# Windowed attention and two MLPs on one core: stores over two queues, exchanged accumulation banks, and three changes of order

## The chip, the core and the metric

The kernel runs on one core of one Trainium2 chip. A core has the engines TensorE (PE in the profile, its weight loads PEld), VectorE (DVE), ScalarE (ACT), GpSimd (POOL) and SyncE (SP), which here only issues transfers. Engines work side by side and wait for each other by semaphores; each takes its own instructions in order. The metric is the device time of one execution in microseconds, lower is better.

## The reference, cut to what matters

```python
def _attn_ref(q, k, v):                      # batch 4, heads 8, seq 576, head_dim 64
    scores = scale * np.matmul(q, k.transpose(0, 1, 3, 2))
    bias = slopes[:, None, None] * (-np.abs(rel))[None]
    mask = (rel >= 0) & (rel < 128)          # rel = query position - key position
    scores = np.where(mask, scores + bias[None], -1e9)
    attn = softmax(scores)
    return np.matmul(attn, v)

x = attention output, one row of 512 for each of the 2304 tokens
h = x @ w_in;  x = where(h > 0, h, exp(min(h, 0)) - 1) @ w_out      # first MLP, 512 -> 2048 -> 512
h = x @ w_in2; out = maximum(0.01 * h, h) @ w_out2                  # second MLP
```

## The kernel before, in words

**Numbers.** All MLP products are made of three matmuls with operands split in a high and a low part (`split_mm`), so that float32 accuracy is kept. The weights are split on the chip, one piece of 128 hidden columns at a time, by steps on ACT and DVE (`w_a1` to `w_lo`, lines 162 to 196): `w_hi` is the cast on ACT (line 189), `w_lo` two subtractions on DVE.

**Attention.** The 2304 tokens are nine blocks of 256, the heads four pairs. A pair of a block is two *steps*; a step is a tile of 128 queries (or tiles of 64 where a sequence of 576 ends and the next begins, in the blocks 2, 6 and 7) with both heads. A step goes: score matmuls, `score_min` on DVE (bias, row minimum, the two halves of the window folded into one), `score_exp` on ACT, `score_rec` (reciprocal) on DVE, `score_norm` on POOL (tile `t`), `transposes` on TensorE into a bank and a copy of it by ACT to tile `pt` (two buffers), `selects` on POOL (the folded part is split again into previous and own keys, in `pt`), `values` on TensorE into `av_ps`, then `values_cast` on ACT and `values_rest` on DVE, which make the high and low part of the MLP's input `x`.

**Banks.** PSUM has eight banks of 512 float32 columns, named by tags here: `y0` to `y3` (sums of the MLP's second product), `s0` and `s1` (scores), `h` and `c`. In the first MLP the hidden sums `h_ps` go alternately into `h` and `c` by the parity of the chunk, transposes into `s1` and `h`, the attention output `av_ps` into `c`.

**Opening** (lines 583 to 616). The first 16 steps run before any MLP work, in an order that is kept as written on every engine (`Ordered`). In round n: the transposes of step n, the values of step n-1, scores of step n+3, the reciprocal of step n+1, the minimum of step n+2, the normalization of step n+1, the exponentials of step n+2, the selects of step n. Up to round 13 the normalization stands ahead of the selects on POOL's queue; in rounds 14 and 15 behind them. Between them stand weight steps of the first pieces (`EARLY`).

**First MLP** (lines 631 to 651). The tokens are five blocks J (512, 256, 512, 512, 512). A block goes through 16 chunks c of 128 hidden columns: `mlp1_h` makes h (12 matmuls, then exponential on ACT, and minimum, maximum, cast and remainder on DVE and ACT), and two chunks later `mlp1_y` adds it into the four sums y. During the blocks 0 to 3, chunks in `starts` also carry attention for a later block: the transposes of a new pair of steps, the values of the pair before, selects, and the scores of the pair after. These are the chunks 3, 7, 11 and 15 of block 0 and every even chunk of the blocks 1 to 3. From here on a scheduler orders the instructions of ACT, DVE, POOL and SP; TensorE keeps the written order.

**End of a block.** The four sums y are copied to `ys` (odd ones by DVE, even ones by ACT; three buffers under tag `eg`, which the activations of both MLPs use too) and stored to `x2T` in DRAM, from where the second MLP loads them. The stores are issued by SP for the first three blocks and by ACT for the last two. Block 4 runs interleaved with the first chunks of the second MLP, whose first activation is `g` (line 681).

Of the kernel before, what the change touches and what calls it, by code (L numbers as in the profile page):

```python
# [20 lines left out]
B, H, S, D = 4, 8, 576, 64  # L21
# [24 lines left out]
FIRST = 16  # L46
# [38 lines left out]
def attention_elu_leaky_kernel(  # L85
# [11 lines left out]
    nc = tc.nc  # L97
# [158 lines left out]
    steps = []  # L256
# [186 lines left out]
    def values(s):  # L443
        if s >= NS:
            return
        st = steps[s]
        j, p = st["j"], st["p"]
        _, v, chunks = QKV[j, p]
        J = max(i for i, (t0, _) in enumerate(BLK1) if t0 <= j * BLK)
        if st["first"] and p == 0 and j * BLK == BLK1[J][0]:  # L450
            x1 = x1p.tile([P, 2, NK, 2 * BLK], F32R, tag="x1", name="x1")
            X1[J] = x1[:, 0], x1[:, 1]
        xh, xl = X1[J]

        early = j < RAW
        pt = st["pt"]
        if st["first"]:
            AV[p] = psp.tile([P, 512], F32, tag=f"y{p % 2}" if early else "c", name="av_ps")
        av, off = AV[p], -j * BLK
        mms = []  # L460
        for t0, n, hh, k0, nk, c in st["parts"]:
            ch = [x[0] for x in chunks].index(k0)
            nth = sum(x[0] == -nk and x[2] == hh for x in mms)
            mms.append((-nk, nth, hh, ch, slice(t0 + off, t0 + off + n), c))


        mms.sort(key=lambda x: x[:3])
        for i, (nk, _, hh, ch, q, c) in enumerate(mms):
            matmul(av[hh * D:hh * D + D, q], v[:-nk, ch, hh * D:hh * D + D], pt[:-nk, c],
                   start=st["first"] and all(x[2] != hh for x in mms[:i]),  # L470
                   stop=st["last"] and all(x[2] != hh for x in mms[i + 1:]), skip_group_check=True)
        st["out"] = None
        if st["last"]:
            o = slice(j * BLK - BLK1[J][0], j * BLK + BLK - BLK1[J][0])
            st["out"] = xh[:, p, o], xl[:, p, o], av[:, :BLK]
# [12 lines left out]
    def mlp1_h(J, cs, late_work=lambda: None):  # L488

        n = BLK1[J][1]
        xh, xl = X1[J]

        last = J == len(BLK1) - 1
        tag = "s0" if last and cs[0] < LAG2 and (LAG2 - cs[0]) % 2 else "h"
        if not last and cs[0] % 2 == (J == 0):

            tag = "c"  # L500
        ps = psp.tile([P, len(cs), n], F32, tag=tag, name="h_ps")
        ws = [weights(1, c, 0) for c in cs]

        late = NK - 1 if cs[0] == 0 else NK
        order = [(ci, kk) for ci in range(len(cs)) for kk in range(late)]
        order += [(ci, kk) for ci in range(len(cs)) for kk in range(late, NK)]
        for ci, kk in order:
            wih, wil = ws[ci]
            s = slice(kk * P, (kk + 1) * P)
            if (ci, kk) == (0, late):  # L510
                late_work()

            split_mm(ps[:, ci, :], wih[:, s], wil[:, s], xh[:, kk, :n], xl[:, kk, :n],
                     ci == 0 and kk == 0, kk == NK - 1, skip_group_check=True)

        g, hi, lo = (pool.tile([P, 2 * BLK], dt, tag=t, name=t)
                     for pool, t, dt in ((egp, "eg", F32), (glp, "gh", F32R), (glp, "gl", F32R)))
        ps = ps.rearrange("p c n -> p (c n)")
        m = len(cs) * n
        nc.scalar.activation(g[:, :m], ps, AF.Exp)  # L520
        nc.vector.tensor_scalar(g[:, :m], g[:, :m], 1.0, -1.0, op0=ALU.min, op1=ALU.add)  # L521
        nc.vector.tensor_tensor(g[:, :m], ps, g[:, :m], op=ALU.max)  # L522
        nc.scalar.copy(hi[:, :m], g[:, :m])  # L523
        nc.vector.tensor_tensor(lo[:, :m], g[:, :m], hi[:, :m].bitcast(F32), op=ALU.subtract)  # L524
        return hi, lo
# [3 lines left out]
    def mlp1_y(J, cs, gg):  # L529
        gh, gl = gg  # L530
        t0, n = BLK1[J]
        per = 512 // n
        if cs[0] == 0:
            Y[J] = [psp.tile([P, per, n], F32, tag=f"y{i}", name=f"y{i}") for i in range(NK // per)]
        for ci, i, m in [(ci, i, m) for ci in range(len(cs)) for i in range(3) for m in range(NK)]:
            woh, wol = weights(1, cs[ci], 1)
            w, g = ((woh, gh), (woh, gl), (wol, gh))[i]

            matmul(Y[J][m // per][:, m % per, :], w[:, m * P:(m + 1) * P], g[:, ci * n:ci * n + n],
                             start=cs[ci] == 0 and i == 0 and m % per == 0, stop=cs[ci] == NC - 1 and i == 2,  # L540
                             skip_group_check=True)
        if cs[-1] == NC - 1:
            for i, y in enumerate(Y.pop(J)):
                ys = egp.tile([P, per, n], F32, tag="eg", name="ys")
                if i % 2:
                    nc.vector.tensor_copy(ys, y)  # L546
                else:
                    nc.scalar.copy(ys, y)

                q = nc.sync if J < len(BLK1) - 2 else nc.scalar  # L550
                q.dma_start(out=x2T[:, i * per:i * per + per, t0:t0 + n], in_=ys)


# [40 lines left out]
    for n in range(FIRST):  # L594
        m = n + 2
        transposes(n, "ch"[n % 2])
        values_to(n - 1)
        if n + 3 < FIRST + 2:
            score_mm(n + 3)
        score_rec(m - 1)  # L600
        if n >= 2:
            values_cast(n - 2)
        score_min(m)
        if n < FIRST - 2:
            score_norm(m - 1)
        score_exp(m)
        selects(n)
        if n >= FIRST - 2:
            score_norm(m - 1)
        if n >= 2:  # L610
            values_rest(n - 2)
        w_early(n)
# [15 lines left out]
    for J in range(len(BLK1) - 1):  # L628
        t0, n = BLK1[J + 1]
        todo = NPAIR * (t0 + n) // BLK - done  # L630
        starts = [i * NC // todo + (3 if J == 0 else 0) for i in range(todo)]
        for c in range(NC):
            if c in starts:
                transposes(2 * done + 1, "s1")
                transposes(2 * done, "h")
                values_to(2 * done - 1)
                if J == 0:

                    w_tick(NC)
                for i in (1, 0):  # L640
                    selects(2 * done + i)
                scores(done + 1)
                done += 1
            elif c == 0 and J:
                values_to(2 * done - 1)
            g = mlp1_h(J, [c], first_late if c == 0 and J == 0 else lambda: None)
            if len(pend) == Y_LAG:
                mlp1_y(*pend.pop(0))
            if at["c"] < NC and c + 1 not in starts:
                w_tick(NC)  # L650
            pend.append((J, [c], g))
# [152 lines left out]
```

## Time and profile before

| | us |
|---|---|
| median of three runs | 944.99 (943.14 to 945.45) |
| the profiled execution, whole | 949.66 |
| its span, first to last instruction | 948.0 |
| TensorE busy | 923.8 (97%) |
| DVE busy | 408.8 (43%) |
| ACT busy | 405.0 (43%) |
| POOL busy | 115.6 (12%) |
| mean granted clock of TensorE | 0.988 of full speed |

All times in the views count from the start of the span. [...] A busy share is an average over stages: the opening lasts until about 47 us, the first MLP with attention until about 450, the first MLP's last block with the beginning of the second MLP until about 590, and the rest is the second MLP alone. A row of the timeline merges like instructions that follow each other; `x12` is their number, and what stands in brackets is how long the engine stood idle before them and what it then waited for.

### The profile page before, as it was taken

The numbers are of one execution on the slowest core, as the hardware profiler recorded it, in microseconds if no ns is written. First come the engines' busy times: TensorE is split into PE (matmuls) and PEld (weight loads), VectorE is DVE, ScalarE is ACT, GpSimd is POOL, SyncE is SP. The second block draws the span as 40 slices with busy tenths as digits, with TensorE's granted clock in tenths as the row PEclk, the third lists the DMA queues.
The fourth block names the chain that finished last, engine by engine and source line by source line (L and its number), as shares of the span: only waits on it lengthen the run. The fifth ranks groups of instructions, "written<-read, shape, count | busy, mean of one in ns | idle before, by whom it ended". The sixth has DMA issues, their size and how long they took to land.

```text
span 948.0 us, 12963 instructions
## 1 busy us (share of the span) xinstructions
PE 923.8 (97%) x4885; PEld 752.4 (79%) x4885; DVE 408.8 (43%) x1035; ACT 405.0 (43%) x918; POOL 115.6 (12%) x281
## 2 busy tenths in 40 slices
PE   8799999999999999999999998999999999999998
PEld 5468887998877777787888887888888888888886
DVE  5878965656544444443476665211211121111111
ACT  6877864444343443332376665322322232222222
POOL 4611122322222211221000000000000000000000
PEclk9979999999999999999999998999999999999999
DMA  9940422321210120100444334010110010001001
GB/s 287 353 174 16 141 67 69 89 67 49 65 45 23 43 82 27 46 9 1 156 157 146 124 128 157 1 67 1 45 44 1 1 45 1 0 1 45 1 1 45
DMA packets 41759, 66.77 MB, mean 70 GB/s; under 512 B 3680, under 2 KB 27232, under 8 KB 41696
## 3 DMA queue, kind: packets, MB, share of 16 engines
q1 hardware_dynamic: 40400, 63.72, 20.2%
q10 hardware_dynamic: 1296, 2.23, 0.6%
q8 instruction: 38, 0.62, 0.3%
q14 instruction: 25, 0.20, 0.1%
HBM read 56.49 MB, written 9.44 MB: 70 GB/s over the span
## 4 chain that ended last, share of the span: by engine, by line
PE 90%; ACT 3%; DMA 3%; DVE 2%; issue 1%; SPq 1%; POOL 0%; ACTq 0%; DVEq 0%
PE h_ps L120 42%; PE y L120 20%; PE o_y L120 18%; PE av_ps L120 3%; PE s_ps L120 2%; DMA wraw<-in_w_in 2%; PE pt_ps L411 2%; PE o_s L120 1%; PE o_c L120 1%; ACT pt L417 1%; DVE x L111 1%; DMA x2T<-ys 1%; ACT wraw L175 0%; ACT x L111 0%; ACT t L111 0%
## 5 line engine op out<-in xcount | busy, mean ns | idle before, releaser
L120 PE MATMUL h_ps<-x,w 128*128 128x512 f32 (+1 forms) x1920 | 431.4, 374 | 8.8 <-DVE x L111 3.7
L120 PEld LDWEIGHTS h_ps<-x,w 128*128 128x128 f32 x1920 | 340.0, 191 | 80.7 <-DVE x L111 12.2
L686 DVE TENSOR_TENSOR g2l<-g,g2h 128x512 fp32r<-128x512 f32 (+1 forms) x80 | 51.0, 637 | 270.1 <-ACT g2h L685 270.1
L120 PE MATMUL o_y<-w,g2h 128*128 128x512 f32 x512 | 157.9, 389 | 0.0
L120 PE MATMUL y<-gh,w 128*128 128x512 f32 (+1 forms) x640 | 157.5, 368 | 0.0
L681 ACT ACTIVATE g<-h_ps 128x512 f32<-128x512 f32 (+1 forms) x80 | 44.2, 554 | 255.9 <-PE h_ps L120 255.9
L120 PEld LDWEIGHTS y<-gh,w 128*128 128x128 f32 x640 | 113.9, 189 | 20.4 <-DVE ys L546 0.3
L120 PEld LDWEIGHTS o_y<-w,g2h 128*128 128x128 f32 x512 | 96.4, 188 | 20.1
L120 PE MATMUL o_y<-w,g2l 128*128 128x512 f32 x256 | 99.6, 389 | 0.0
L520 ACT ACTIVATE eg<-h_ps 128x512 f32<-128x512 f32 (+1 forms) x80 | 44.0, 551 | 88.8 <-PE h_ps L120 86.2
L111 ACT ACTIVATE t<-t,stat 128x128 f32<-128x128 f32 (+2 forms) x160 | 62.6, 394 | 45.3 <-DVE t L111 30.3
L111 POOL TENSOR_SCALAR t<-t,stat 128x128 f32<-128x128 f32 (+3 forms) x160 | 66.9, 431 | 101.1 <-DVE stat L111 91.3
L120 PE MATMUL y<-gl,w 128*128 128x512 f32 (+1 forms) x320 | 78.7, 368 | 0.0
L523 ACT CAST gh<-eg 128x512 fp32r<-128x512 f32 (+1 forms) x80 | 46.2, 578 | 74.2 <-DVE eg L522 67.5
L111 POOL TENSOR_SCALAR_AFFINE_SELECT pt<-pt 128x256 f32<-128x256 f32 (+1 forms) x112 | 47.2, 429 | 221.0 <-ACT pt L417 217.2
L524 DVE TENSOR_TENSOR gl<-eg,gh 128x512 fp32r<-128x512 f32 (+1 forms) x80 | 51.3, 641 | 38.8 <-ACT gh L523 38.6
L120 PEld LDWEIGHTS y<-gl,w 128*128 128x128 f32 x320 | 56.9, 189 | 10.0
L521 DVE TENSOR_SCALAR eg<-eg 128x512 f32<-128x512 f32 (+1 forms) x80 | 32.6, 408 | 72.1 <-ACT eg L520 70.1
L120 PEld LDWEIGHTS o_y<-w,g2l 128*128 128x128 f32 x256 | 48.0, 188 | 10.0
L111 DVE CUSTOM_DVE_ANT_0 t<-s_ps,bias 128x256 f32<-128x256 f32 (+4 forms) x160 | 51.8, 370 | 2.9 <-PE s_ps L120 2.8
L522 DVE TENSOR_TENSOR eg<-h_ps,eg 128x512 f32<-128x512 f32 (+1 forms) x80 | 50.9, 638 | 2.5
L685 ACT CAST g2h<-g 128x512 fp32r<-128x512 f32 (+1 forms) x80 | 46.3, 578 | 2.3
(58 smaller groups left out, 678.7 us busy)
## 6 DMA issues: line engine op xcount, KB each, us to landing
wraw<-in_w_in SPq DMA_DIRECT2D x32, 512.0 KB, 3.8
wraw<-in_w_out SPq DMA_DIRECT2D x32, 512.0 KB, 4.8
qkr<-in_kT SPq DMA_DIRECT2D x28, 192.0 KB, 2.9
xr<-x2T SPq DMA_DIRECT2D x4, 1024.0 KB, 5.4
qkr<-in_qT SPq DMA_DIRECT2D x28, 128.0 KB, 2.6
out<-os SPq DMA_DIRECT2D x14, 256.0 KB, 2.2
vr<-in_vp SPq DMA_DIRECT2D x16, 192.0 KB, 2.5
x2T<-ys SPq DMA_DIRECT2D x10, 256.0 KB, 2.3
```

The source lines that it names most:

```text
L111: ins = f(*args, **kw)
L120: tc.keep_in_program_order(nc.tensor.matmul(*args, **kw))
L411: tc.keep_in_program_order(nc.tensor.transpose(ps[:nk, col:col + n], t[:n, c:c + nk], ident[:n, :n]))
L417: tc.keep_in_program_order(nc.scalar.copy(pt[:nk, c], ps[:nk, c]))
L520: nc.scalar.activation(g[:, :m], ps, AF.Exp)
L521: nc.vector.tensor_scalar(g[:, :m], g[:, :m], 1.0, -1.0, op0=ALU.min, op1=ALU.add)
L522: nc.vector.tensor_tensor(g[:, :m], ps, g[:, :m], op=ALU.max)
L523: nc.scalar.copy(hi[:, :m], g[:, :m])
L524: nc.vector.tensor_tensor(lo[:, :m], g[:, :m], hi[:, :m].bitcast(F32), op=ALU.subtract)
L681: nc.scalar.activation(g, ps, AF.Prelu, alpha=0.01)
L685: nc.scalar.copy(hi, g)
L686: nc.vector.tensor_tensor(lo, g, hi.bitcast(F32), op=ALU.subtract)
```

## The change

Five edits in one diff:

1. `mlp1_y`: of the stores of the blocks 3 and 4, those of the odd sums (copied by DVE) are issued by SP, those of the even sums by ACT as before.
2. `values`: within a step the matmuls with few key rows (64) come before those with 128.
3. `mlp1_h`: the banks `h` and `c` change places in the blocks 0 to 3. In a chunk of `starts`, h now goes into `h`; in the chunk after it (in block 0, in the even ones) into `c`.
4. Opening: in round 14 the normalization of step 15 stands ahead of the exponentials and the selects, as in the rounds before; only round 15 keeps the other order.
5. First MLP: of the two steps of a new pair, the one with fewer tiles is transposed first into `s1`, and with equal numbers the earlier one; before it was always the later one.

```diff
--- before.py
+++ after.py
@@ -460,13 +460,13 @@
         mms = []
         for t0, n, hh, k0, nk, c in st["parts"]:
             ch = [x[0] for x in chunks].index(k0)
-            nth = sum(x[0] == -nk and x[2] == hh for x in mms)
-            mms.append((-nk, nth, hh, ch, slice(t0 + off, t0 + off + n), c))
+            nth = sum(x[0] == nk and x[2] == hh for x in mms)
+            mms.append((nk, nth, hh, ch, slice(t0 + off, t0 + off + n), c))
 
 
         mms.sort(key=lambda x: x[:3])
         for i, (nk, _, hh, ch, q, c) in enumerate(mms):
-            matmul(av[hh * D:hh * D + D, q], v[:-nk, ch, hh * D:hh * D + D], pt[:-nk, c],
+            matmul(av[hh * D:hh * D + D, q], v[:nk, ch, hh * D:hh * D + D], pt[:nk, c],
                    start=st["first"] and all(x[2] != hh for x in mms[:i]),
                    stop=st["last"] and all(x[2] != hh for x in mms[i + 1:]), skip_group_check=True)
         st["out"] = None
@@ -495,7 +495,7 @@
 
         last = J == len(BLK1) - 1
         tag = "s0" if last and cs[0] < LAG2 and (LAG2 - cs[0]) % 2 else "h"
-        if not last and cs[0] % 2 == (J == 0):
+        if not last and cs[0] % 2 != (J == 0):
 
             tag = "c"
         ps = psp.tile([P, len(cs), n], F32, tag=tag, name="h_ps")
@@ -547,7 +547,7 @@
                 else:
                     nc.scalar.copy(ys, y)
 
-                q = nc.sync if J < len(BLK1) - 2 else nc.scalar
+                q = nc.sync if J < len(BLK1) - 2 or i % 2 else nc.scalar
                 q.dma_start(out=x2T[:, i * per:i * per + per, t0:t0 + n], in_=ys)
 
 
@@ -601,11 +601,11 @@
         if n >= 2:
             values_cast(n - 2)
         score_min(m)
-        if n < FIRST - 2:
+        if n < FIRST - 1:
             score_norm(m - 1)
         score_exp(m)
         selects(n)
-        if n >= FIRST - 2:
+        if n == FIRST - 1:
             score_norm(m - 1)
         if n >= 2:
             values_rest(n - 2)
@@ -631,8 +631,9 @@
         starts = [i * NC // todo + (3 if J == 0 else 0) for i in range(todo)]
         for c in range(NC):
             if c in starts:
-                transposes(2 * done + 1, "s1")
-                transposes(2 * done, "h")
+
+                for s, tag in zip(sorted((2 * done, 2 * done + 1), key=lambda s: len(steps[s]["subs"])), ("s1", "h")):
+                    transposes(s, tag)
                 values_to(2 * done - 1)
                 if J == 0:
 
```

The order of the instructions as built, at three places. First POOL in the opening, rounds 13 to 15; `pt_642`, `pt_679` and `pt_715` are the tiles of the steps 13, 14 and 15, `t_627` and `t_663` those of the steps 14 and 15:

```order
 L111 TENSOR_SCALAR t_627<-t_627,stat_628 128x128 x2
 L111 AFFINE_SELECT pt_642<-pt_642 128x256 x2
+L111 TENSOR_SCALAR t_663<-t_663,stat_664 128x128 x2
 L111 AFFINE_SELECT pt_679<-pt_679 128x256 x2
-L111 TENSOR_SCALAR t_663<-t_663,stat_664 128x128 x2
 L111 AFFINE_SELECT pt_715<-pt_715 128x256 x2
 L111 TENSOR_SCALAR t_696<-t_696,stat_697 64x128 x2
```

The normalization of step 15 moved ahead of the two selects of step 14; nothing else on POOL moved here.

Second ACT and SP at the stores of block 4; `ys_5755`, `5758`, `5761` and `5764` are the copies of y0 to y3, `g2_5790` and `g2_5817` are activations of the second MLP. ACT before:

```order
L548 COPY ys_5755<-y0_4815 128x512
L548 COPY ys_5761<-y2_4817 128x512
L551 DMA x2T_81<-ys_5755 128x512
L551 DMA x2T_81<-ys_5758 128x512
L551 DMA x2T_81<-ys_5761 128x512
L551 DMA x2T_81<-ys_5764 128x512
L170 ACTIVATE wf_5770<-wraw_5767 128x1024
L175 ACTIVATE wraw_5767<-wraw_5767 128x1024
L681 ACTIVATE g2_5790<-h2_ps_5777 128x512
L681 ACTIVATE g2_5817<-h2_ps_5804 128x256
```

ACT of the change:

```order
L548 COPY ys_5755<-y0_4815 128x512
L548 COPY ys_5761<-y2_4817 128x512
L551 DMA x2T_81<-ys_5755 128x512
L551 DMA x2T_81<-ys_5761 128x512
L170 ACTIVATE wf_5770<-wraw_5767 128x1024
L175 ACTIVATE wraw_5767<-wraw_5767 128x1024
L682 ACTIVATE g2_5790<-h2_ps_5777 128x512
L682 ACTIVATE g2_5817<-h2_ps_5804 128x256
```

SP of the change:

```order
L665 DMA xr_6092<-x2T_81 128x4x512
L159 DMA wraw_5796<-in_w_in2 128x1024
L159 DMA wraw_5796<-in_w_out2 128x1024
L551 DMA x2T_81<-ys_5758 128x512
L551 DMA x2T_81<-ys_5764 128x512
L665 DMA xr_6615<-x2T_81 128x4x512
L721 DMA out_0<-os_6064 128x512
```

Two issues left ACT's queue, and stand on SP's behind the last weight loads and ahead of the next load of `x2T`.

Third TensorE at the start of a pair in block 2 (chunk 10), with the engines that a first instruction waits for; `t_3207` is the earlier, `t_3218` the later step. Before:

```order
L411 MATMUL pt_ps_3301<-ident_82,t_3218 128x64 [waits Pool_49] x2
L411 MATMUL pt_ps_3301<-ident_82,t_3218 64x64 [waits Pool_49] x2
L411 MATMUL pt_ps_3309<-ident_82,t_3207 128x128 [waits DVE_49]
L411 MATMUL pt_ps_3309<-ident_82,t_3207 128x128
L120 MATMUL av_ps_3314<-pt_3174,vr_2929 64x128 [waits DMAHW2_49]
...
L120 MATMUL s_ps_3338<-qkr_3189 128x256 [waits PE_49,Activation_49]
...
L120 MATMUL h_ps_3373<-x1_1807,w1_10_1243 128x512 [waits DVE_49]
```

Of the change:

```order
L411 MATMUL pt_ps_3301<-ident_82,t_3207 128x128 [waits Pool_49] x2
L411 MATMUL pt_ps_3306<-ident_82,t_3218 128x64 [waits DVE_49,Pool_49]
L411 MATMUL pt_ps_3306<-ident_82,t_3218 128x64 [waits Pool_49]
L411 MATMUL pt_ps_3306<-ident_82,t_3218 64x64 [waits Pool_49] x2
L120 MATMUL av_ps_3314<-pt_3166,vr_2929 64x128 [waits DMAHW2_49,DVE_49]
...
L120 MATMUL s_ps_3338<-qkr_3189 128x256 [waits Activation_49]
...
L120 MATMUL h_ps_3373<-x1_1807,w1_10_1243 128x512 [waits PE_49,Activation_49]
```

The two transposed tiles changed places, h waits for ACT (the copy out of bank `h`) and no longer for DVE, and the wait for DVE stands at the attention output instead.

## Rows read from the trace of the kernel before

**Rows 1.** Waits of TensorE (PE), whole run: engine, line, waited for: us, times, longest.

```profile
PE h_ps L120 <- DVE x L111: 3.7, 8, 1.2
...
PE pt_ps L411 <- POOL t L111: 3.3, 3, 2.3
PE h_ps L120 <- ACT g L681: 3.3, 1, 3.3
```

**Rows 2.** The same view, 8 to 45 us only.

```profile
PE av_ps L120 <- POOL pt L111: 3.6, 8, 0.8
```

**Rows 3.** Windows: us, busy PE, PEld, DVE, ACT, POOL, granted clock (PEclk), DMA, GB/s.

```profile
40.00:45.00 5.00, 3.44 (x34) 2.26 (x34) 3.69 (x18) 3.92 (x16) 3.11 (x6) 1.00 1.02 410
45.00:50.00 5.00, 4.27 (x16) 3.08 (x17) 1.93 (x8) 2.96 (x9) 3.92 (x11) 0.51 1.01 403
...
586.00:590.00 4.00, 4.00 (x11) 3.03 (x11) 3.22 (x6) 3.74 (x5) 0.00 (x0) 0.50 0.00 0
```

**Rows 4.** Timeline, opening: start us, us, engine, line, operation, [idle before <-releaser].

```profile
42.13 0.17 DVE L111 RECIPROCAL stat<-stat 128x2 f32<-128x2 f32 x1 [0.85 <-ACT stat L111]
...
43.02 0.36 ACT L417 COPY pt<-pt_ps 128x256 f32<-128x256 f32 x1
...
43.30 1.28 DVE L111 TENSOR_TENSOR w<-wraw,w 128x512 fp32r<-128x512 f32 x2
...
43.44 1.88 POOL L111 TENSOR_SCALAR_AFFINE_SELECT pt<-pt 128x256 f32<-128x256 f32 x2 [1.75 <-ACT pt L417]
...
45.30 0.72 POOL L111 TENSOR_SCALAR t<-t,stat 128x128 f32<-128x128 f32 x2
...
45.73 0.82 PE L411 MATMUL pt_ps<-ident,t 128*128 128x128 f32 x2 [2.25 <-POOL t L111]
...
47.53 4.21 PE L120 MATMUL h_ps<-x,w 128*128 128x512 f32 x9
```

**Rows 5.** The selects in place of tile pt on POOL, 8 to 48 us.

```profile
L111 POOL TENSOR_SCALAR_AFFINE_SELECT pt<-pt x24: 406/407/1400, 11.1 to 47.5; 128x256 f32<-128x256 f32 x24
```

**Rows 6.** Timeline, first h chunks.

```profile
51.67 0.76 PE L120 MATMUL av_ps<-pt,qkvr 128*64 128x128 f32 x8
...
52.90 6.65 PE L120 MATMUL h_ps<-x,w 128*128 128x512 f32 x27 [0.47 <-ACT x L111]
```

**Rows 7.** Timeline around one pair's start in the first MLP.

```profile
358.25 2.88 PE L120 MATMUL h_ps<-x,w 128*128 128x512 f32 x12
...
362.32 0.69 DVE L522 TENSOR_TENSOR eg<-h_ps,eg 128x512 f32<-128x512 f32 x1
...
364.44 1.39 PE L120 MATMUL av_ps<-pt,vr 128*64 128x128 f32 x16
...
365.94 0.63 ACT L417 COPY pt<-pt_ps 128x256 f32<-128x256 f32 x2 [0.21 <-PE av_ps L120]
...
366.88 0.42 DVE L111 TENSOR_TENSOR x<-av_ps,x 128x256 fp32r<-128x256 f32 x1 [2.49 <-ACT x L111]
...
367.36 3.01 PE L120 MATMUL h_ps<-x,w 128*128 128x512 f32 x12 [0.56 <-DVE x L111]
```

**Rows 8.** Timeline, stores of the last first-MLP block.

```profile
575.46 0.43 SPq L159 DMA_DIRECT2D wraw<-in_w_out  x1
...
576.71 6.12 ACTq L551 DMA_DIRECT2D x2T<-ys  x4
...
581.77 0.69 DVE L546 COPY ys<-y 128x512 f32<-128x512 f32 x1 [4.77 <-DMA x2T<-ys]
...
584.91 0.86 ACT L681 ACTIVATE g<-h_ps 128x512 f32<-128x512 f32 x2
...
585.55 5.49 PE L120 MATMUL h_ps<-x,w 128*128 128x512 f32 x12 [3.28 <-ACT g L681]
```

**Rows 9.** The first two of these stores, tile ys, 577 to 577.5 us.

```profile
L551 ACTq DMA_DIRECT2D x2T<-ys x2: 327/386/444, 576.7 to 577.1; - x2
...
DMA to landing us min/median/max: 4.9/5.1/5.2
```

## The prediction

> **What bounds the kernel now.** The order of reading is: TensorE's own waits, the granted clock where those waits are long, the timeline around each, and last the landing times of the transfers. TensorE's whole list of waits is short, its four largest entries being [rows 1, 2]: no engine but TensorE is the bound, and a change can only win by taking away its idle time or the slow clock that follows it. Three of the four are touched by this change. [...] The three places:
>
> *Opening, step 14.* TensorE stops for 2.25 us, from 43.48 to 45.73, on the normalization of step 15 by POOL [rows 4]. POOL had idled until 43.44, did two selects until 45.32, and only then the normalization, although its input, the reciprocal, was there at 42.30 [rows 4]. The next nine h matmuls then take 4.21 us, against 2.16 at the rate of 2.88 for twelve [rows 4, 7].
>
> *First MLP, chunks that start a pair.* The h matmuls go into bank c, which the attention output left a moment ago: they wait for its cast on ACT and its subtraction on DVE, 8 times, 3.7 us [rows 1]. In the example av ends at 365.83, the subtraction at 367.30, h starts at 367.36 after 0.56 us of idleness [rows 7].
>
> *Last first-MLP block's stores.* ACT issues four stores between 576.71 and 582.83 [rows 8]. The fourth waits for a DVE copy that itself waits 4.77 us for an earlier store to land, and everything behind it on ACT stands. The activation that frees bank h starts at 584.91, TensorE loses 3.28 us, from 582.27 to 585.55, and the next twelve matmuls take 5.49 us in place of 2.88 [rows 7, 8].
>
> **The change part by part.**
>
> *Stores by two queues.* Removed from ACT: two issues, each with a wait on DVE. ACT is then free after its second copy and its second issue, near 577.5. It has still the two weight steps before the activation; in the profile they took it from 582.83 to 584.91, 2.1 us [rows 8], so it is ready near 579.6. The activation's buffer is that of store 1 (the tag has three buffers, and four stores go round them), so store 1 must have landed. It was issued at 577.1 and took 5.2 us: 582.3 [rows 9]. SP can issue it as early: its last weight load is out at 575.89 [rows 8]. For the landing I take 582.3 again, as the same bytes are in flight; the bounds are a wait that vanishes (landing at 581.6, as store 0 did after 4.9 us) and one as long as now. TensorE restarts 0.64 us after the activation's start (584.91 to 585.55), so at 582.95: idle 0.68 instead of 3.28, gain 2.6. That is shorter than the longest wait that the clock survived (0.8), so the slow clock goes too: 5.49 - 2.88 = 2.6. Sum **5.2 us**. A reader may hope that a queue of its own gets store 1 landed sooner, which would take the last 0.68 away as well. [...] What is late next: DVE still stands until store 0 lands, and the weight steps and g2l behind it come no sooner than now; the readers of g2l, the o_y matmuls, follow a whole h group, which is their cover. On SP nothing that is due stands behind the new issues: only the next x2T load and the output stores. For the block before, TensorE shows no wait at its stores, so nothing is counted there.
>
> *Normalization ahead of selects.* In the order it now stands before the selects of step 14. POOL is idle by then and needs 0.72 us from 42.30 [rows 4]: 43.1, before the selects' input is copied at 43.38. So it costs the selects nothing, and the transposes of step 15 run at once. The values of step 14 then wait for the selects. The first one takes 1.40 us where the median is 0.407 [rows 5], beside two DVE subtractions from 43.30 to 44.58 [rows 4]; I keep 1.40, since neither moves. [...] So the second select ends at 45.32 as before. From there: half of the value matmuls (0.38 of the 0.76), nine h at 2.16, values of step 15 at 0.76, the cast wait of 0.47 [rows 6]: 45.32 + 0.38 + 2.16 + 0.76 + 0.47 = 49.09, where the trace has 52.90 [rows 6]. **3.8 us**. This needs the clock to stay up: the wait is now cut in two, some 0.9 us (43.48 and half of the 0.82 that the two transposes took at the slow clock, to 44.84) and a bit, between 0.8 that left the clock alone and 2.25 that did not, nearer to the former. With the slow clock the nine cost 4.21 and the term is 1.8. ACT and DVE, which are nearly full just after, start that stretch on the values of step 15, so they move forward with TensorE; that cover is why I count the whole term.
>
> *Banks of h exchanged.* In a starting chunk h now takes bank h, which the second pair of transposes used: it waits for their copies by ACT, which stand before the cast on ACT's queue. In the example they end at 366.57, TensorE is free at 366.80 (367.36 - 0.56) [rows 7]: no wait. Bounds: the whole 3.7, or 3.7 less the copies' 0.63 where no score matmuls fill the gap, as after the last pair. I take **3.2 us**. The next chunk takes c, and the attention output after it must wait for that chunk's DVE maximum: done at 363.01, needed at 364.44 [rows 7], 1.4 us of cover. Before, the transposes into h, some 0.8 us earlier, needed the same maximum, so the wait is looser than the one it replaces.
>
> *Order of transposes and short rows first.* Where both steps have as many tiles the earlier step is now transposed first; its copy needs one buffer of the two, freed by the earlier step's values, so ACT starts half a values group sooner. It lies beside TensorE's score matmuls: nothing. Short rows first changes the order of equal matmuls in three of nine blocks, and all of TensorE's 8 waits of values on POOL lie in the opening [rows 2], whose tiles are all of 128 rows: nothing.
>
> **Sum:** 5.2 + 3.8 + 3.2 = 12.2 us. The profiled execution took 949.66 us (span 948.0), so 937.5 there; it lies 4.67 above the median of the runs, 944.99, from which the same 12.2 gives **932.8**.
>
> **The rivals.**
> 1. *The clock falls in the opening all the same.* For it: 0.9 us of standing still is longer than any wait that the clock survived there. Against: work stands between the two halves. It costs 2.0: 934.8. Chance 0.17.
> 2. *The normalization gets caught beside the DVE subtractions* and ends where it does now. Against: 1.0 us of room before 43.30. The opening gives nothing: 936.6. Chance 0.05. [...]
> 3. *Store 1 lands late,* because on SP's queue it stands behind the weight loads. For it: the last of them goes out 1.6 us before [rows 8, 9]. If it lands at 584.9 or later the stall and the slow clock stay: 12.2 - 5.2 = 7.0, 938.0. Chance 0.12.
> 4. *A new stall in the first block.* The scheduler put a weight cast on ACT ahead of the exponentials of the first score pair and of an h activation, at a place where ACT is full. Priced like the end's stall, 3.28 + 2.6: 938.7. Chance 0.08.
> 5. *Slower: bank c becomes the short one.* Each of the 28 starts sends its attention output into c, one chunk after h left it; in the block of 256 columns the cover is smaller than 1.4 us. It decides from (12.2 + 2.8)/28 = 0.54 us for each start; at 0.7 it is 19.6 - 12.2 = 7.4 slower, 952.4. Against: the same maximum now has an earlier reader, and TensorE's list shows next to no wait for it. Chance 0.03.
> 6. *It moves nothing that counts,* each gain being taken by the next late engine: about 944. Chance 0.05.
>
> **How the numbers follow.** The forecast has 0.50; its own range is 930 to 935, from the runs' spread of 2.3 us and the 0.68 and 0.5 left in the terms. The range goes from 929 to 940, past rivals 1 to 4, and leaves out 5, 6 and the tails. About 0.3% (2.8 us) is what a measurement of this kernel can tell from no change. Faster: the forecast and rivals 1 to 4, 0.92; the same 0.05; slower 0.03.
>
> **What the profile of the changed kernel would show.** Right: no TensorE wait on POOL t of over 1 us near 43 and a clock of 1.00 from 45 to 50; the first h group's second part starting near 49; the entry of h on DVE x gone; near 582 a wait under 1 us, no slow twelve matmuls, ACT's store issues two and short. Wrong: a clock near 0.5 after 45; TensorE waiting at 582 on the activation for 3 us; av waiting on DVE eg through the first MLP; new TensorE waits from 50 to 75.

## The result, and the profile after

The changed kernel takes **934.91 us** (median; 934.25 to 935.24, four runs) against 944.97 (943.14 to 945.45, four runs) before: ratio 0.9895, 95% interval 0.9879 to 0.991. It is 10.06 us faster; 932.8 was forecast, with 929 to 940 as the range. Its profiled execution took 935.24 us.

The span and the first part of the page, busy time by engine:

```profile
span 933.5 us, 13059 instructions
...
PE 915.7 (98%) x4885; PEld 749.1 (80%) x4885; DVE 408.9 (44%) x1035; ACT 405.0 (43%) x918; POOL 118.3 (13%) x281
```

TensorE was idle for 933.5 - 915.7 = 17.8 us; before it was 948.0 - 923.8 = 24.2. Of the 14.5 us between the two spans 6.4 are idle time and 8.1 are busy time, though TensorE has the same 4885 matmuls: most of that part is its clock, whose mean granted level is 0.998 here and was 0.988 there.

TensorE's waits in the changed kernel (engine, line, waited for: us, times, longest), to be read beside [rows 1, 2]:

```profile
PE av_ps L120 <- POOL pt L111: 4.8, 9, 1.2
...
PE pt_ps L411 <- POOL t L111: 1.5, 2, 1.1
PE h_ps L120 <- ACT g L682: 1.5, 1, 1.5
...
PE h_ps L120 <- ACT pt L417: 0.5, 1, 0.5
PE y L120 <- DVE ys L546: 0.5, 1, 0.5
```

The entry of h on DVE x, 3.7 us in eight waits, is gone, and in its place stands one wait of 0.5 on ACT's copies. The wait of 3.3 on g is 1.5. The wait of 2.3 on POOL t near 43 us is gone; the 1.1 that this entry still has is another one, at 7 us (0.7 before), and near 44 us TensorE now waits 1.2 on the selects instead. The last line is new: a wait of the next block's y on a copy to `ys`.

Timeline of the opening in the changed kernel (start us, us, engine, line, operation, idle before), which answers to [rows 4, 6]:

```profile
42.33 0.17 DVE L111 RECIPROCAL stat<-stat 128x2 f32<-128x2 f32 x1 [0.85 <-ACT stat L111]
...
42.60 0.72 POOL L111 TENSOR_SCALAR t<-t,stat 128x128 f32<-128x128 f32 x2 [0.71 <-DVE stat L111]
...
43.50 1.28 DVE L111 TENSOR_TENSOR w<-wraw,w 128x512 fp32r<-128x512 f32 x2
43.51 0.38 PE L411 MATMUL pt_ps<-ident,t 128*128 128x128 f32 x2
...
43.66 1.86 POOL L111 TENSOR_SCALAR_AFFINE_SELECT pt<-pt 128x256 f32<-128x256 f32 x2 [0.35 <-ACT pt L417]
...
45.10 0.91 PE L120 MATMUL av_ps<-pt,qkvr 128*64 128x128 f32 x8 [1.21 <-POOL pt L111]
...
45.94 2.35 PE L120 MATMUL h_ps<-x,w 128*128 128x512 f32 x9
...
49.35 1.43 PE L120 MATMUL h_ps<-x,w 128*128 128x512 f32 x4 [0.47 <-ACT x L111]
```

The normalization runs right behind the reciprocal, the transposes follow without a wait, the wait of 1.21 us is now that of the values on the selects, and the nine h matmuls take 2.35 us where they took 4.21.

The stores of the last first-MLP block in the changed kernel, which answer to [rows 8]:

```profile
566.90 4.32 PE L120 MATMUL h_ps<-x,w 128*128 128x512 f32 x24
567.04 0.81 ACTq L551 DMA_DIRECT2D x2T<-ys  x2
567.37 5.90 SPq L551 DMA_DIRECT2D x2T<-ys  x2
...
572.22 0.69 DVE L546 COPY ys<-y 128x512 f32<-128x512 f32 x1 [4.88 <-DMA x2T<-ys]
...
573.47 0.88 ACT L682 ACTIVATE g<-h_ps 128x512 f32<-128x512 f32 x2 [3.39 <-DMA x2T<-ys]
...
574.12 3.01 PE L120 MATMUL h_ps<-x,w 128*128 128x512 f32 x12 [1.51 <-ACT g L682]
```

ACT issues its two stores in 0.81 us instead of 6.12. It then does its two weight steps and stands for 3.39 us on the landing of a store that holds the buffer of g.

### The profile page after: what moved, and what is told of

Same layout as the page of the kernel before. It is cut to its first block, busy times and chain, and to the rows that moved or that the text cites. A ratio compares the mean times of both kernels' runs of the same rounds, so it can differ in the third digit from the quotient of the medians.

```text
span 933.5 us, 13059 instructions
## 1 busy us (share of the span) xinstructions
PE 915.7 (98%) x4885; PEld 749.1 (80%) x4885; DVE 408.9 (44%) x1035; ACT 405.0 (43%) x918; POOL 118.3 (13%) x281
## 4 chain that ended last, share of the span: by engine, by line
PE 90%; DMA 3%; ACT 3%; DVE 2%; issue 1%; SPq 1%; POOL 0%; ACTq 0%; DVEq 0%
PE h_ps L120 41%; PE y L120 20%; PE o_y L120 19%; PE s_ps L120 4%; PE av_ps L120 3%; DMA wraw<-in_w_in 2%; PE pt_ps L411 1%; PE o_s L120 1%; PE o_c L120 1%; DMA x2T<-ys 1%; ACT wraw L175 1%; ACT wf L170 1%; DVE wraw L111 1%; ACT t L111 0%; DVE t L111 0%
## 5 line engine op out<-in xcount | busy, mean ns | idle before, releaser
L120 PE MATMUL h_ps<-x,w 128*128 128x512 f32 (+1 forms) x1920 | 426.1, 371 | 3.4 <-ACT g L682 1.5
L111 POOL TENSOR_SCALAR t<-t,stat 128x128 f32<-128x128 f32 (+3 forms) x160 | 69.1, 446 | 99.5 <-DVE stat L111 89.2
```

Source lines behind the costliest of these rows:

```text
L111: ins = f(*args, **kw)
L120: tc.keep_in_program_order(nc.tensor.matmul(*args, **kw))
```

## The experiments

**The kernel before, once more (no edit).** Against which clock is the gain to be reckoned?

> The kernel before, unchanged, looked at once more with a profile. The profiled execution of before took 949.66 us where its plain runs took 944.97; that of the changed kernel 935.24 against 934.91. Theory: the slow clock after the two long waits of before (windows 45 to 50 and 586 to 590) is there in every execution; then this look shows 0.5 in both windows again and takes about 945 to 950. Rival: whether the clock falls after such a wait differs from execution to execution; then this look lacks one of the two slow stretches, and is 2 to 5 us shorter than 949.66.

It took 945.35 us with its profile, near the median. Span and busy time:

```profile
span 943.6 us, 12963 instructions
...
PE 919.4 (97%) x4885; PEld 749.7 (79%) x4885; DVE 409.1 (43%) x1035; ACT 404.8 (43%) x918; POOL 117.3 (12%) x281
```

The idle time is 943.6 - 919.4 = 24.2 us, the same as in the first profile of this kernel; the busy time is 4.4 us less. The rows at the two stalls, and between them those at one of the waits on DVE x (timeline of TensorE):

```profile
46.65 0.68 PE L411 MATMUL pt_ps<-ident,t 128*128 128x128 f32 x2 [2.27 <-POOL t L111]
...
47.86 3.86 PE L120 MATMUL h_ps<-x,w 128*128 128x512 f32 x9
...
52.78 1.43 PE L120 MATMUL h_ps<-x,w 128*128 128x512 f32 x4 [0.47 <-ACT x L111]
...
66.33 3.02 PE L120 MATMUL h_ps<-x,w 128*128 128x512 f32 x12
...
71.90 2.88 PE L120 MATMUL h_ps<-x,w 128*128 128x512 f32 x12
...
434.54 3.02 PE L120 MATMUL h_ps<-x,w 128*128 128x512 f32 x12 [1.21 <-DVE x L111]
...
573.32 4.32 PE L120 MATMUL h_ps<-x,w 128*128 128x512 f32 x24
...
582.21 4.29 PE L120 MATMUL h_ps<-x,w 128*128 128x512 f32 x12 [3.19 <-ACT g L681]
```

The waits are those of the first profile. The slow clock behind them is shorter: from 45 to 50 us it is 0.78 where it was 0.51 [rows 3], and the twelve matmuls after the wait on g take 4.29 us, not 5.49 [rows 8]. So the profile from which the forecast took its prices was an unusual execution: 949.66 us, and of 58 further runs of this kernel one was as long (949.81). All that follows is held against this second profile.

**Edit 1 alone: stores by two queues.**

```diff
-                q = nc.sync if J < len(BLK1) - 2 else nc.scalar
+                q = nc.sync if J < len(BLK1) - 2 or i % 2 else nc.scalar
```

> Before, with the stores of the odd sums on SP and nothing else. Theory (each edit works in its own place): the changed kernel's trace has TensorE wait 1.51 us there where before has 3.28, and no slow clock after it, so 1.8 + 2.5 = 4.3 us less than before in the trace. Rival (the plain runs of before do not all have the slow clock there): about 1.8 us less. A further rival: nothing, the wait only moves to the transfer: 0.

943.97 us (939.44 to 945.31, 12 runs), ratio 0.9979 [0.9965, 0.9993]. TensorE at the stores:

```profile
581.04 3.01 PE L120 MATMUL h_ps<-x,w 128*128 128x512 f32 x12 [1.41 <-ACT g L681]
```

In its profile the place gives what it gives in the full change: a wait of 1.41 for 3.19, and no slow matmuls (the clock is 1.00 from 580 to 585 us), together 3.06 us; the span is 3.2 shorter. The runs lie in clusters (near 942.0 and near 944.0), so the median, 0.7 below that of the kernel before, tells little; the ratio, which goes by all runs, is worth 0.0021 x 945 = 2.0 us, with 0.7 to 3.3 as its interval.

**Edit 4 alone: one normalization ahead of the selects.**

```diff
-        if n < FIRST - 2:
+        if n < FIRST - 1:
...
-        if n >= FIRST - 2:
+        if n == FIRST - 1:
```

> Before, with the normalization of step 15 ahead of the selects of step 14 and nothing else. Theory: the clock stays up from 45 to 50 and the second part of the first h group starts near 49.4 instead of 52.9: 3.5 us less, and up to 1.8 more if the later slow stretch near 65 shortens too. Rival: the plain runs of before lose only the wait and not the clock, so the gain is 1.0 to 1.5. Rival: ACT and DVE, nearly full from 53 to 66, set the pace and give it back: 0.

943.41 us (941.38 to 946.68, 11 runs), ratio 0.9984 [0.9971, 0.9996]. TensorE in the opening and at the stores:

```profile
46.69 2.35 PE L120 MATMUL h_ps<-x,w 128*128 128x512 f32 x9
...
50.10 4.14 PE L120 MATMUL h_ps<-x,w 128*128 128x512 f32 x16 [0.47 <-ACT x L111]
...
580.38 4.60 PE L120 MATMUL h_ps<-x,w 128*128 128x512 f32 x12 [4.04 <-ACT g L681]
```

The opening ends 2.68 us earlier (52.78 to 50.10), but in this profile the stall at the stores is 0.85 longer (3.19 to 4.04); the stores landed later, the longest after 6.1 us, where the repeated kernel before has 5.3. TensorE's idle time, 24.0 us, is where it was.

**Edit 3 alone: banks exchanged.**

```diff
-        if not last and cs[0] % 2 == (J == 0):
+        if not last and cs[0] % 2 != (J == 0):
```

> Before, with the banks h and c exchanged and nothing else. Theory: TensorE's waits of h on DVE x (3.7 us) go, with the slower first matmuls after each; 3 to 4 us less. Rival: h waits for the copies by ACT instead, which here still wait for the values of both steps, since the order of the transposes is the old one: 1 us or less gained.

939.95 us (936.86 to 942.89, 7 runs), ratio 0.9942 [0.992, 0.9964]: the largest single part. The same windows (us, busy PE, PEld, DVE, ACT, POOL, clock, DMA, GB/s), first of the kernel before (repeated), then with the banks exchanged:

```profile
72.00:300.00 228.00, 226.93 (x1465) 189.68 (x1464) 142.02 (x430) 118.39 (x325) 57.14 (x135) 1.00 0.21 66
300.00:450.00 150.00, 146.55 (x824) 116.28 (x824) 66.51 (x202) 54.38 (x158) 28.52 (x70) 1.00 0.12 35
```

```profile
72.00:300.00 228.00, 227.93 (x1485) 190.96 (x1483) 141.26 (x429) 117.75 (x325) 55.85 (x135) 1.00 0.21 66
300.00:450.00 150.00, 149.53 (x832) 119.50 (x829) 69.13 (x209) 56.31 (x164) 28.28 (x70) 1.00 0.16 49
```

TensorE's idle time in these 378 us falls from 4.5 to 0.5 us. The clock is 1.00 on both sides, so this is all waiting. From the h of chunk 4 to the 24 h matmuls at the stores the stretch is 501.42 us before and 496.00 with the banks exchanged: 5.42 less, of which 4.0 is idle time.

**Edits 2 and 5 alone: short rows first, order of the transposes.**

```diff
-            mms.append((-nk, nth, hh, ch, slice(t0 + off, t0 + off + n), c))
+            mms.append((nk, nth, hh, ch, slice(t0 + off, t0 + off + n), c))
...
-                transposes(2 * done + 1, "s1")
-                transposes(2 * done, "h")
+                for s, tag in zip(sorted((2 * done, 2 * done + 1), key=lambda s: len(steps[s]["subs"])), ("s1", "h")):
+                    transposes(s, tag)
```

> Before, with the two changes of order alone (which step is transposed first, short rows first in values). Theory: both lie beside other work; within 1 us of before. Rival: with the earlier step's transposes first, the copy waits for the values of one step and not of both, so that the cast and subtraction behind it on ACT and DVE come sooner and part of the 3.7 us of waits of h on DVE x goes even with the old banks: 1 to 2 us less.

945.16 us (940.73 to 949.08, 12 runs), ratio 1.0001 [0.9985, 1.0018]: nothing that can be measured, though its profile shows h waiting on DVE x for 2.2 us in four waits where it was 3.7 in eight.

**The kernel before with 14 more idle matmuls in the opening's long wait.** They multiply the identity and nobody reads them; they fill most of the wait that edit 4 removes.

```diff
-            warm(ps[:, :BLK], WARM[1])
+            warm(ps[:, :BLK], 18 if s == FIRST - 1 else WARM[1])
```

> Before, with 14 more idle matmuls on TensorE (2.1 us of work that nobody reads) in the opening's 2.3 us wait for the normalization of step 15. The wait for the data stays as long; only the idleness in it goes. Theory (the slow clock after this wait follows the idleness, in most executions but not in all): the windows 45 to 50 show 1.00, the nine h matmuls take 2.2 to 2.4 instead of 3.6 to 4.2, and the plain runs are 1 to 2 us shorter. Rival (the clock falls for another reason there): 3.6 to 4.2 for the nine again, and no change of the time.

944.84 us (942.65 to 947.75, 12 runs), ratio 1.0003 [0.9991, 1.0014]. In the profile the wait is 0.73, the nine h matmuls take 2.33 us, and the clock from 45 to 50 us is 1.00 (0.78 in the repeated kernel before); the runs are no shorter, although in this profile the second part of the first h group comes 1.99 us earlier (50.79 for 52.78). To hold the clock at this one place is worth nothing measurable; whether the other runs lose the gain later, or seldom had the slow clock here, no trace shows.

**The full change without edit 1** (the diff of edit 1, the other way round).

> The changed kernel with the stores put back on ACT. e1 gave 0.7 us for the stores alone, where the trace shows 1.7 less waiting and a slow stretch less. Theory (the gains add, their sizes set by how often the clock falls): 0.7 to 4.3 above the changed kernel, 936 to 939. Rival (the stores are worth something only together with the other edits, or nothing): the same as the changed kernel, 934.9.

939.56 us (938.13 to 940.31, 5 runs), ratio 0.9939 [0.9926, 0.9952]. TensorE at the stores:

```profile
576.00 5.49 PE L120 MATMUL h_ps<-x,w 128*128 128x512 f32 x12 [3.36 <-ACT g L681]
```

Here the stores' edit is worth 939.56 - 934.91 = 4.65 us, and the row agrees: 3.36 + 5.49 against 1.51 + 3.01 in the full change, 4.33 us.

**Edits 1 and 3 together** (their two diffs).

> Edits 1 and 3 alone: exchanged banks and stores by two queues. Alone the banks gave 939.95 us and the stores 0.7 us; inside the full change the stores are worth 4.6 (939.56 without them, 934.91 with). Theory A: what makes the stores worth more is the exchange of the banks, because without it the time saved at the stores is lost again in slow clock: about 939.95 - 4.5 = 935.5 us. Theory B: the two are independent, and the stores give 0.7 as they did alone: about 939.2 us; then it is the opening that the stores need. Both theories expect the wait of h on g near 1.5 us at the end.

936.42 us (933.88 to 938.03, 6 runs), ratio 0.9898 [0.9878, 0.9918]. By medians theory A comes closer: 939.95 - 936.42 = 3.5 us for the stores, not 0.7. But the 0.7 that both theories start from was such a median of clusters. By the ratios the two edits give 2.0 and 5.5 us alone and 9.6 together; the difference of 2.1 is no larger than the intervals (1.3, 2.1 and 1.9 us to either side). Whether the banks make the stores worth more is not settled; at the stores the profiles with and without exchanged banks have nearly the same rows (a wait of 1.24 and of 1.41, then 3.06 and 3.01 us).

**The changed kernel, once more** (no edit).

> The changed kernel once more, with a second profile. It should give 934.9 us again (934.2 to 935.3). Theory A (whether the clock falls after a wait of about 1.6 us is chance): the wait of the scores of about 1.6 us near 61.6 us is there again, and the granted clock from 60 to 65 us may be 1.00 this time. Theory B (the fall is fixed by the work): it is 0.76 again, as in the first profile.

935.17 us (934.32 to 935.37, 5 runs), ratio 0.9887 [0.9869, 0.9906]. TensorE's idle time is 933.3 - 915.6 = 17.7 us, 0.1 from the first profile. After the wait for the copy `pt` near 61 us the clock fell again; from 60 to 65 us it was 0.81, and 0.76 in the first profile:

```profile
61.49 1.18 PE L120 MATMUL s_ps<-qkr 64*64 64x192 f32 x10 [1.57 <-ACT pt L417]
62.60 4.60 PE L120 MATMUL h_ps<-x,w 128*128 128x512 f32 x12
```

Theory B stands for this pair; two of the runs below qualify it.

**The full change with own buffers for the last two copies of the sums.**

```diff
-                ys = egp.tile([P, per, n], F32, tag="eg", name="ys")
+                if J == len(BLK1) - 1 and i >= 2:
+                    ys = glp.tile([P, per, n], F32, tag=("gh", "gl")[i % 2], name="ys")
+                else:
+                    ys = egp.tile([P, per, n], F32, tag="eg", name="ys")
```

> The changed kernel, with the last block's third and fourth store copied into buffers of another tag, so that neither a copy nor the next activation waits for a store to land. What is left in the changed kernel's trace is a wait of 1.51 us of TensorE on that activation (574.12), of which 3.39 us on ACT were for a store's landing. Theory: that wait goes, 1.5 us less, 933.4; more if the clock sometimes falls there. Rival (SP or DVE is late by as much anyway): no change.

933.22 us (932.61 to 933.75, 4 runs), ratio 0.9875 [0.9862, 0.9888]. ACT and TensorE at the stores:

```profile
569.97 0.61 ACT L684 ACTIVATE g<-h_ps 128x512 f32<-128x512 f32 x1
...
571.86 0.38 ACT L684 ACTIVATE g<-h_ps 128x256 f32<-128x256 f32 x1 [1.28 <-DMA x2T<-ys]
...
572.41 2.88 PE L120 MATMUL h_ps<-x,w 128*128 128x512 f32 x12
```

The first activation, which frees the bank for TensorE, no longer needs the buffer of a store in flight, TensorE does not wait, and the twelve matmuls take 2.88 us. The second activation still waits 1.28 us for a landing, which TensorE does not feel. So what was left of this stall in the changed kernel was the landing of a store ahead of the first activation.

**The full change with the two DVE subtractions one round later.**

```diff
-         (10, "a1", 2), (11, "a2", 2), (11, "ts", 2), (12, "add", 2), (13, "hi", 2), (14, "lo", 2),
+         (10, "a1", 2), (11, "a2", 2), (11, "ts", 2), (12, "add", 2), (13, "hi", 2), (15, "lo", 2),
```

> The full change, and the two DVE subtractions that lay beside the selects of step 14 moved one round later. Theory A (the select is held up by them): the two selects take about 0.82 us in all in place of 1.86, the wait of the values near 44 us falls from 1.21 us to about 0.3, and the time falls by about 1 us where DVE does not become late elsewhere: 933.9 us. Theory B (they only move the same delay to the selects of step 15, or make the weights late): the wait appears at the values of step 15, and the time stays at 934.9 us or rises.

933.17 us (932.69 to 933.47, 5 runs), ratio 0.9869 [0.9849, 0.9889]. POOL and TensorE:

```profile
43.72 0.88 POOL L111 TENSOR_SCALAR_AFFINE_SELECT pt<-pt 128x256 f32<-128x256 f32 x2 [0.34 <-ACT pt L417]
...
44.19 0.92 PE L120 MATMUL av_ps<-pt,qkvr 128*64 128x128 f32 x8 [0.23 <-POOL pt L111]
...
48.60 0.51 PE L120 MATMUL h_ps<-x,w 128*128 128x512 f32 x1 [0.62 <-ACT x L111]
...
60.94 1.18 PE L120 MATMUL s_ps<-qkr 64*64 64x192 f32 x10 [1.34 <-ACT pt L417]
62.04 3.06 PE L120 MATMUL h_ps<-x,w 128*128 128x512 f32 x12
```

The two selects take 0.88 us in place of 1.86. That shows that the subtractions held them up, as theory A has it; the runs gain 1.7 us, more than its 1. The profile gains 0.67 us at once (49.27 to 48.60); another 1.54 come at 62 us, where the clock stayed up this time (1.00 from 60 to 65 us against 0.81, and 3.06 us against 4.60).

**Both of these in the full change.**

> The full change with own buffers for the last two copies of the sums (which gave 933.22 us) and the two DVE subtractions one round later. If the two gains add up: about 932.3 us; if the subtractions only move their delay: 933.2 us; above 934 us only if the moved subtractions make a weight piece late.

932.65 us (931.91 to 932.81, 4 runs), ratio 0.9861 [0.984, 0.9881]: the lowest median of all, though within the spread of the two runs before it. Its profile has the smallest idle time, 15.2 us, but the clock fell near 61 us (0.77 from 60 to 65) behind the same kind of wait that left it at 1.00 in the run before:

```profile
60.99 1.18 PE L120 MATMUL s_ps<-qkr 64*64 64x192 f32 x10 [1.36 <-ACT pt L417]
62.09 4.62 PE L120 MATMUL h_ps<-x,w 128*128 128x512 f32 x12
```

Up to there the two kernels give TensorE the same work. So the fall at this place is not fixed by the work. It is more frequent with the change, though: it came in five of the six profiles that hold all of the edits 2 to 5, and in one of the eight others. Why is open: with the banks exchanged the wait there is as long as in the full change (1.58 us), and the clock stayed at 1.00 from 60 to 70 us.

All profiles side by side (idle is the span less PE's busy time):

| edits | median us | span | PE busy | PE idle |
|---|---|---|---|---|
| none, first profile | 944.97 | 948.0 | 923.8 | 24.2 |
| none, repeated | 944.67 | 943.6 | 919.4 | 24.2 |
| 1 | 943.97 | 940.4 | 918.0 | 22.4 |
| 4 | 943.41 | 941.7 | 917.7 | 24.0 |
| 3 | 939.95 | 935.8 | 915.7 | 20.1 |
| 2, 5 | 945.16 | 939.0 | 915.8 | 23.2 |
| none, idle matmuls | 944.84 | 941.7 | 918.9 | 22.8 |
| 1, 3 | 936.42 | 935.1 | 916.9 | 18.2 |
| all but 1 | 939.56 | 938.6 | 918.3 | 20.3 |
| all | 934.91 | 933.5 | 915.7 | 17.8 |
| all, repeated | 935.17 | 933.3 | 915.6 | 17.7 |
| all, own buffers | 933.22 | 931.7 | 915.1 | 16.6 |
| all, subtractions later | 933.17 | 931.0 | 914.2 | 16.8 |
| all, both of these | 932.65 | 931.1 | 915.9 | 15.2 |

A profiled execution need not be a middle one: with edits 2 and 5 it took 940.73, the shortest of its twelve.

## Why the prediction was right, and which of its steps were off

The time came out inside the range and by the mechanisms named, 2.1 us above the number. That it is so near is in part luck, since errors of both signs cancel: the stores gave 2.2 us less than forecast, 1.4 were lost from 50 to 70 and 0.4 lacked in the opening, while the banks' stretch gave 1.2 more and the end 0.7 that was not forecast. Where the gain lies is read by laying the marks of the changed kernel beside those of the kernel before, repeated; both are near their medians, and their spans differ by 10.1 us, as the runs do:

| mark | before, repeated | after | gained in the stretch that ends here |
|---|---|---|---|
| second part of the first h group | 52.78 | 49.35 | 3.43 |
| h of chunk 4 | 71.90 | 69.83 | -1.36 |
| the 24 h matmuls at the stores | 573.32 | 566.90 | 4.35 |
| end of the twelve behind the wait on g | 586.50 | 577.13 | 2.95 |
| end of the span | 943.6 | 933.5 | 0.7 |

*Opening, 3.8 us forecast.* Right in place, and in size against the profile that it was priced on: the forecast put the second part at 49.09; the changed run stands 0.20 later from the start (reciprocal at 42.33 for 42.13 [rows 4]), so 49.29, and it came at 49.35. Against the repeated kernel before it is less: of the 3.43 some 0.7 were there ahead of the edit's place (the last idle matmuls at 43.77 and 43.06), and 2.7 are left, as in the run of edit 4 alone. Rivals 1 and 2 did not come: the clock was 1.00 from 45 to 50, and the normalization ran before the subtractions.

*Given back from 50 to 70, not forecast.* The wait of the scores on ACT's copy near 61 us was there before as well, but the repeated kernel before kept its clock behind it (1.00 from 65 to 70 us, and 3.02 us for twelve h matmuls) and the changed one lost it (0.76 from 60 to 65, and 4.54). That takes 1.5 us back. The profile that the forecast was priced on had lost it too (0.56 from 65 to 70 us), behind a wait of 1.77, and the prediction says nothing of this slow stretch. First that profile, then the changed kernel:

```profile
65.33 1.85 PE L120 MATMUL s_ps<-qkr 64*64 64x192 f32 x10 [1.77 <-ACT pt L417]
...
67.11 5.45 PE L120 MATMUL h_ps<-x,w 128*128 128x512 f32 x12
```

```profile
61.59 1.20 PE L120 MATMUL s_ps<-qkr 64*64 64x192 f32 x10 [1.58 <-ACT pt L417]
62.72 4.54 PE L120 MATMUL h_ps<-x,w 128*128 128x512 f32 x12
...
69.83 2.88 PE L120 MATMUL h_ps<-x,w 128*128 128x512 f32 x12
```

Rival 4 had the region right (new loss in the first block) with another mechanism, a stall on ACT: the wait itself got shorter, 1.58 for 1.79.

*Banks, 3.2 us forecast.* Too small: 4.35 in the trace of the full change, 5.42 in that of this edit alone, 4.7 by the medians of its runs. The whole upper bound of 3.7 came; ACT's copies cost only the one wait of 0.5. What the forecast left out is busy time: behind each of the eight waits the twelve matmuls take about 0.13 us longer (3.02 for 2.88 with 512 columns, 1.70 for 1.59 with 256), about 1 us together. That is nearly all of the 1.0 by which TensorE's busy time falls in this stretch with the full change. Rival 5 is out: no wait of the attention output on DVE appears.

*Order and short rows, nothing forecast.* Right in the runs. The trace has 1.0 us less idle time, which they don't show.

*Stores, 5.2 us forecast.* The mechanism is right: ACT is free at once, the activation then waits for a landing, TensorE's wait falls from over 3 us to 1.5, and the slow matmuls are gone (the clock is 1.00 from 570 to 580 us). Mis-sized are two terms. The landing was taken as 5.2 us [rows 9]; in the changed kernel the longest of these stores took 5.9, and the wait is 1.51 instead of 0.68: rival 3 in small, and the sign "near 582 a wait under 1 us" did not come. SP's queue did not land the store of y1 sooner: it took 5.7 us there, where the first two on ACT's queue had taken 4.9 and 5.2 [rows 9]. And the 2.6 us for the slow clock were those of one execution; the repeated profile has 4.29 - 2.88 = 1.4. The reason given for the term, that 0.8 was the longest wait that the clock survived, is a misreading too (0.8 is the longest of [rows 2], which end at 45 us): the wait of 1.2 in [rows 1], at 437.78 us, left the clock at 1.00. A little comes on top: 0.4 of the last 0.7 in the table is slow clock behind the twelve (0.79 from 585 to 590 us before, 1.00 from 575 to 580 after), from whose end the next h group is 2.92 us away before and 2.56 after.

*Stores of the block before, nothing counted.* Wrong by 0.7 us. With the stores over two queues the last copy to `ys` by DVE waits longer for a landing (2.31 us in the full change, 1.65 without edit 1), and TensorE waits 0.5 on that copy near 454 us. The wait stands in all seven profiles that hold edit 1 and in none of the others. From the h of chunk 4 to the 24 h matmuls edit 1 makes the stretch longer in each of three pairs: by 0.70 alone (501.42 to 502.12), by 0.69 with the banks (496.00 to 496.69), by 0.66 in the full change (496.41 to 497.07). So the 4.35 in the table are some 5.0 from the other edits less this.

**The step that failed is the last one**, "it lies 4.67 above the median of the runs, 944.99, from which the same 12.2 gives 932.8". The 4.67 us by which that execution lay above the median were themselves slow clock: idle time is equal in both profiles of the kernel before, busy time differs by 4.4 us. The first profile loses more than the repeated one in three stretches: 1.0 us in the opening behind the transposes, 1.3 behind the wait on g, and 3.1 from the scores at 65 us to the h of chunk 4, less some 1 us by which it was ahead at the transposes. The first two stretches were priced, so 2.3 of the 12.2 us were a loss that the median does not have. What only an unusual execution loses can't be won back from the median. With the rows of the repeated profile the same steps give: opening 52.78 - (49.09 + 0.92) = 2.8, since that run stands 0.92 later at the transposes; stores 3.19 - 0.68 + 1.41 = 3.9; banks 3.2; together 9.9, and so 935.1. A second profile would have shown this before the change was made. That 935.1 lies so close to the 934.91 measured is luck again: this sum too has nothing for the loss from 50 to 70, and puts the stores about 1 us too high and the banks about 1 us too low.

*Do the parts make the whole?* By their ratios the edits alone give 2.0 (stores), 1.5 (normalization), 5.5 (banks) and -0.1 us (order, short rows), 8.9 together, and the full change 9.9. The difference is within the intervals, so the runs show no need for an effect of one part on another. The single edits' runs lie in clusters, up to 6 us apart (936.9 and 942.9 with the banks alone). Within one kernel the shorter ones have the higher mean clock, 0.998 and 0.992 there, and 0.006 of some 936 us is 5.6 us, so the clock can account for nearly all of it; in which stretches those runs lost it no trace shows.

## What to carry to other kernels

Compare the span less TensorE's busy time first: it came out the same to 0.1 us in the two kernels that were profiled twice, while busy time for the same matmuls differed by 4.4. Price a wait in full, but the slow clock behind it by a second profile, and check that the profiled execution is near the median before carrying a sum from one to the other. Before moving a store to another queue, look at what else is waiting for its buffer: here the queue gave 2.0 us alone and 4.7 within the full change, although it cost 0.7 at the block before, and the buffer gave the next 1.7.

## What the runs showed of the hardware that was not expected

Whether TensorE's clock falls behind a wait (as to 0.50 of full speed from 586 to 590 us [rows 3]) differs from execution to execution of the same work. In windows of 0.2 us the first profile shows 1.00 from 43.4 to 45.0, 0.72 in the next and 0.50 in the one after, so that 0.72 is a mean of both levels. The two profiles of the kernel before show it near 65 us: twelve h matmuls took 5.45 us behind a wait of 1.77 in one and 3.02 behind a wait of 1.79 in the other, with a clock of 0.56 and of 1.00 from 65 to 70 us. Behind the opening's wait of 2.25 to 2.27 us, which six of the profiles have, the clock from 45 to 50 us was 0.51, 0.78, 0.73 and 0.75 in four and 1.00 in two. Windows of the kernel before (repeated) and of the one with edits 2 and 5:

```profile
45.00:50.00 5.00, 3.33 (x15) 2.45 (x16) 1.83 (x8) 3.68 (x15) 4.00 (x11) 0.78 1.03 412
```

```profile
45.00:50.00 5.00, 4.10 (x27) 2.72 (x27) 2.10 (x8) 3.02 (x10) 4.07 (x11) 1.00 0.97 388
```

Behind the waits of 3.1 to 4.0 us at the stores it fell in six profiles of seven (the next twelve h matmuls took 4.29 to 5.49 us, and 3.01 in the seventh), behind those of 1.1 to 1.51 there in none of five; near 61 us it fell after a wait of 1.36 in one kernel and stayed after 1.34 in another. So waits of the same length ended either way; what decides it no trace shows.

Two selects on POOL take twice as long beside two subtractions on DVE, 1.86 us against 0.88, shown by moving the subtractions alone. The forecast had kept that price as a given; it was the next microsecond to be had.
